# Attention and MoE on one core: all transposes on TensorE as fp32 words of two tokens, streaming key tiles from -60, a new order

## The chip, the cores and the metric

The kernel runs on 1 core of one Trainium2 chip. The metric is the device time of one execution in microseconds (us). Lower is better.

## What is computed

Attention over 4 batches, 8 heads, 768 tokens and 64 columns a head, then a two-layer MLP with a learned negative slope on the 3072 tokens that come out. Heads 0, 2 and 6 are "retrieval" heads: full causal attention. The other five are "streaming" heads: a token sees the first 4 tokens (sinks) and the last 64.

```python
scores = scale * np.matmul(q, k.transpose(0, 1, 3, 2))
causal = rel >= 0                                  # rel = query position - key position
stream_keep = causal & ((pos[None, :] < n_sink) | ((rel >= 0) & (rel < window)))
mask = np.where(retr, causal, stream_keep)         # n_sink 4, window 64
a = softmax(np.where(mask, scores, -1e9))
x = np.matmul(a, v)                                # [B, H, S, D] -> [B*S, H*D] = [3072, 512]
h = x @ w_in                                       # w_in [512, 2048]
out = (np.maximum(h, 0) + alpha * np.minimum(h, 0)) @ w_out    # w_out [2048, 512]
```

## The kernel before, in words

**Segments.** The attention is cut into 16 segments n: batch n // 4 and one of the head pairs `PAIRS = [(2, 6), (1, 5), (0, 4), (3, 7)]`. So n % 4 = 0 has two retrieval heads, n % 4 = 2 one of each kind, the others two streaming heads. The MLP is cut into 8 token tiles t, two for a batch: 512 tokens (t even) and 256 (t odd).

**Items and their order.** All work is cut into named items, and `ORDER` (line 14) is a list of some 1,080 names written out in full. The program is what comes of calling the items in that order. Each engine runs its own instructions in that order, so the list is the order of every queue: TensorE (PE), VectorE (DVE), ScalarE (ACT), GpSimd (POOL) and SyncE (SP), which issues most DMAs. The names are:
- `Lq`, `Lk`, `Lv` n: load q, k, v of a segment (SP; `load_q`, `load_k`, `load_v`). `Cq`, `Ck`, `Cv`: cast to bf16, on the engine that the strings `CQ`, `CK`, `CV` name (V, P, A).
- `Tq`, `Tk` n (`to_array`, line 355): TensorE transposes q and k of a segment into PSUM. `tq`, `tk` (`put_q` line 365, `put_k` line 373): copies from PSUM into `qT` and `kT`, with the tokens put in order.
- `Dq`, `Dk` n (`dma_q` line 321, `dma_k` line 336): the same by DMA transpose, for segments 8 to 15.
- `S` n.hh.m (`S_retr`, `S_stream`): scores of a part of a head. `s`: their exponential on ScalarE. `m`: multiplication by a 0/1 mask on VectorE, for segments 4 to 15; segments 0 to 3 add a mask of -30000 by a matmul with `ident` instead (lines 462 and 501).
- `A` n.hh (`AV`, line 535): the exponentials times v, with a 65th column of ones that gives the row sum. `a` (`AV_out`): division by the sum into `xn`.
- `X` n: `xn` transposed into `xT`, by TensorE for segments 0 to 3 and 15 (`X_pe`, line 574, then `X_out`, the item `x`), by DMA for the others (`X_dma`, line 567).
- `P` t.f (line 588): first MLP layer for a 512-column slice of PSUM; tile 0's first slices are cut by heads (`P0.f.0` to `P0.f.2`). `p` and `g`: the two halves of the slope function, on ScalarE (line 602) and VectorE (line 609).
- `O` t.s.u (line 613): a quarter of the second layer for 128 tokens. `o`: copy on ScalarE and store. `L0` to `L2`: the last 128 tokens, cut by columns (line 636).
- `warm`: matmuls on zeros, which keep TensorE going while it waits.

**Bursts.** For segments 4 to 15 a score matmul isn't issued at once but pooled (`one_score`, line 411), as long as the next names are scores or items that TensorE doesn't run (`beside_burst`). `emit_burst` (line 417) then issues the pool. With at least 576 columns on each head of the pair, the two heads' matmuls use the two row halves of the array at the same time (line 430). Otherwise each runs by itself over all rows (line 423).

**Tiles.** There are three tilings of queries: `FULL` (6 tiles of 128) for pairs of two retrieval heads, `FAR` (7 tiles, starts 0, 128, 252, ... in steps of 124) in batch 0, and `NEAR` (7 tiles, steps of 112) from batch 1 on. A streaming head's key tile holds the 4 sinks and the keys of a query tile. It gets scores for 192 or 176 queries. The transposed output is kept with the tiling's starts. Rows of q and k lie 6 or 2 tokens to a partition in segments 0 to 7 (`row_tokens`), and `put_q` and `put_k` bring them in order with strided copies (`in_order`). In segments 8 to 15 they lie 1 token to a partition. In batch 0 the sinks of v are copied by `sinks` (line 306), later they are loaded by small DMAs.

**PSUM** has 8 banks, which `take` and `give` hand out in the order of their age. In batch 0 the scores go by bank pairs, `SC2 = [(0, 1), (2, 3)]`.

Of the kernel before, what the change touches and what calls it, by code (L numbers as in the profile page):

```python
# [8 lines left out]
AF = mybir.ActivationFunctionType  # L9
# [5 lines left out]
busy zero id warm0 kz3 Lq0.0 sz1 vz2 nms nmr so1 vz0 Lq0.1 Lk1 warm8 warm5 warm3 kz1 qz0 one Lq1 Lk0 La Ck0.0 kz2  # L15
Cq0.0 Tq0.0 tq0.0 Tk0.0 qz warm2 Lk2 kz0 tk0.0 Ck1.0 Ck1.1 Cq0.1 Tk1 S0.0.1 s0.0.1 Tq0.1 S0.0.0 Cq1 warm7 Lv0 tk1.0
sz2 vz1 vz3 Tq1 Lq2 Ck0.1 S0.0.2 s0.0.0 tk1.1 Tk0.1 Ck2.1 tq1 S1.1.0 s0.0.2 Ck2.0 warm4 tq0.1 nz0 s1.1.0 Cq2 tk0.1 Cv0
Lk3 S0.1.0 kfz0 Lv1 vo ro0 Ck3.1 s0.1.0 Lq3 Ck3.0 wi1 wi0 Cq3 sz0 idf S1.0.0 so2 Al s1.0.0 so0 al S0.1.1 s0.1.1 Lv2
Tq2 Tk2 tk2.1 tk2.0 S0.1.2 S1.0.1 A0.0 s0.1.2 a0.0 Cv1 A0.1 a0.1 Cv2 s1.0.1 tq2 S1.1.1 nz1 Tk3 S2.0.1 tk3.0 s1.1.1
S2.0.2 X0 s2.0.1 x0 wi6 s2.0.2 wi7 Lv3 Lq5 Tq3 tk3.1 S2.0.0 wi5 m4.0.2 warm6 S2.1.0 A1.0 a1.0 Lk4 s2.0.0 A2.0 S2.1.1  # L20
A1.1 a2.0 tq3 s2.1.0 a1.1 S3.0.0 s2.1.1 s3.0.0 A2.1 a2.1 S3.1.1 X1 S3.0.1 s3.0.1 Lk5 wi4 kfz2 Cv3.0 Cq5 Lk7 wi2 X2
Ck4.0 s3.1.1 S3.1.0 x1 P0.0.0 x2 P0.0.1 A3.0 P0.1.0 P0.1.1 Lk6 Lq4 Lq6 Ck4.1 kfz3 nr Cv3.1 s3.1.0 A3.1 Lv7 Lv5 Lq7
Ck5.0 wi3 a3.0 P0.2.0 Tq5 tq5 P0.3.0 P0.3.1 a3.1 X3 x3 ns kfz1 P0.2.1 Tk4 near2 P1.2 P0.1.2 P0.2.2 P0.0.2 p1.2 p0.1
g0.1 Ck5.1 P1.0 P0.3.2 g1.2 P0.15 tk4.0 p0.2 g0.2 p0.15 wo0 p1.0 Lk8 near0 g0.15 g1.0 ro1 P1.12 P1.14 m12.1.2 p0.0
g0.0 wo1 tk4.1 p1.12 P0.14 g1.12 p0.14 g0.14 P0.13 p0.13 g0.13 P0.11 p1.14 Tk5 Ck7.1 g1.14 P1.10 tk5.0 p0.11 p1.10
Ck6.0 Ck7.0 g0.11 m8.0.2 tk5.1 wo2 Lv6 Lv4 P0.10 P0.8 p0.8 Tk7 g1.10 wo3 Cq4 Lk9 P0.12 P1.8 p0.10 g0.8 p0.12 g0.10 Tq4
P0.6 P0.9 p0.3 Ck6.1 g0.3 tq4 P0.4.0 P0.5.0 Tk6 P0.4.1 p1.8 g1.8 tk7.0 p0.9 g0.9 Cq6 P0.5.1 P0.5.2 p0.5 g0.12 p0.6
tk6.1 P0.4.2 g0.6 g0.5 tk6.0 S4.0.5 P0.7 p0.7 P1.6 g0.7 P1.4 s4.0.5 p0.4 Tq6 m4.1.2 tk7.1 g0.4 Cv5 p1.6 g1.6 O0.1.0
tq6 S4.0.3 O0.2.0 O0.2.1 S5.1.1 S5.0.0 S4.0.1 S6.1.0 m14.0.2 p1.4 g1.4 s5.0.0 O0.1.1 s4.0.3 s4.0.1 O0.2.2 S5.0.2
S5.1.0 S4.0.2 S5.1.2 s6.1.0 m4.0.1 Cv7 O0.3.0 s5.0.2 s5.1.2 s5.1.1 s4.0.2 O0.1.2 s5.1.0 O0.1.3 o0.1 Cq7 Cv4 O0.3.1  # L30
m5.1.0 m8.1.2 m5.0.2 m4.0.3 m5.1.2 S4.0.0 S4.1.4 S5.0.1 S4.0.4 S4.1.0 s4.0.4 s5.0.1 Lk10 m5.0.1 O0.2.3 O0.3.2 Tq7
m5.0.0 o0.2 s4.1.0 m4.0.4 m5.1.1 A5.1 s4.0.0 m4.0.0 a5.1 O0.3.3 tq7 S7.0.0 S7.0.1 S4.1.3 S7.1.1 S6.0.5 S4.1.1 m4.0.5
s4.1.4 o0.3 Lq9 s4.1.3 Ck8 m4.1.3 A5.0 a5.0 X5 s4.1.1 A4.0 s7.0.0 s7.1.1 Lk11 Lq8 s7.0.1 a4.0 s6.0.5 near1 m7.0.0
m7.1.1 m4.1.0 O1.1.0 S7.1.0 S6.0.4 S7.0.2 S4.1.5 S6.0.1 S7.1.2 S6.1.1 O1.1.1 Cv6 s7.1.0 O1.0.0 s4.1.5 m7.0.1 s6.1.1
m4.1.5 m6.1.1 s7.1.2 m6.1.0 s7.0.2 m7.0.2 S6.0.2 S4.1.2 S6.1.2 S6.0.0 s6.0.4 s4.1.2 s6.0.1 s6.1.2 O1.0.1 m6.0.5 m7.1.0
m4.1.1 m4.1.4 m7.1.2 m6.1.2 S6.0.3 A4.1 s6.0.0 m6.0.0 m6.0.1 A7.1 O1.1.2 A6.1 s6.0.3 m6.0.4 m6.0.3 s6.0.2 a4.1 a6.1
A6.0 A7.0 a6.0 O1.1.3 O0.0.0 O0.0.1 O0.0.2 O1.0.2 m10.0.2 O1.0.3 O0.0.3 o0.0 X4 X6 a7.1 a7.0 X7 P2.9 P2.3 p2.9 P3.4
Ck9 Cq9 g2.9 P2.14 p2.14 g2.14 Cq8 p3.4 Lq10 Lq11 Dk8.0 P2.10 p2.10 Dk9.1 o1.0 p2.3 g2.3 g3.4 Dk8.1 P3.2 P3.14 P3.12
# [24 lines left out]
s15.1.0 m12.1.4 s14.0.2 s15.1.1 m14.1.1 m14.0.5 m14.1.2 m12.1.3 m14.1.0 A12.1 m14.0.3 A14.1 A14.0 a14.0 s15.1.2 a14.1
m15.0.2 s15.0.1 a12.1 O4.1.1 X13 O4.0.0 O4.0.1 O4.0.2 O4.0.3 m15.0.0 m15.1.1 O4.1.2 m15.0.1 m15.1.2 m15.1.0 A15.0 o4.0
A15.1 a15.0 O4.1.3 a15.1 O5.0.2 X15 O5.0.3 X14 x15 o4.1 o5.0 X12 P6.11 p6.11 P6.2 P6.15 P6.10 p6.10 P7.4 P6.0 P6.1
g6.11 g6.10 p6.1 P6.6 P7.8 p6.15 g6.15 g6.1 p6.0 g6.0 P6.5 p7.4 p6.5 p6.6 g7.4 g6.6 g6.5 P6.3 P6.12 P7.2 p6.3 p6.12
g6.12 p6.2 g6.2 P6.4 p7.8 P7.6 P6.14 g6.3 g7.8 p7.6 p6.4 g7.6 g6.4 P7.10 P6.7 P6.8 p6.8 p6.7 P7.0 P6.9 P6.13 g6.7 p7.2
g7.2 g6.8 p7.10 g7.10 p6.9 P7.14 O6.3.0 P7.12 p6.13 g6.13 p7.12 O6.0.0 O6.0.1 O6.1.0 p7.0 g7.0 g6.9 O6.3.1 O7.0.0
O6.3.2 O6.1.1 p7.14 p6.14 g6.14 g7.12 O6.3.3 o6.3 O6.0.2 O6.1.2 O6.1.3 o6.1 O6.0.3 o6.0 O6.2.0 O6.2.1 O6.2.2 O7.0.1
O7.0.2 O6.2.3 o6.2 m12.0.2 g7.14 L2 l2 O7.0.3 o7.0 L0 L1 l1 warm1 l0  # L70
""".split()


@with_exitstack
def kernel(
    ctx: ExitStack,
    tc: tile.TileContext,
    q: bass.AP,
    k: bass.AP,
    v: bass.AP,  # L80
    is_retrieval: bass.AP,
# [14 lines left out]
    bf16 = DT.bfloat16  # L96

    RETR = [1, 0, 1, 0, 0, 0, 1, 0]
    PAIRS = [(2, 6), (1, 5), (0, 4), (3, 7)]
    NSINK = 4  # L100
    NT = 7
    SLOT = 256
    LAY = 4
    CROSS = 8

    class Tiles:

        def __init__(self, starts, masked):
# [13 lines left out]
    def full(n):  # L122
        return all(RETR[h] for h in PAIRS[n % 4])
# [724 lines left out]
```

## Time and profile before

| what | value |
|---|---|
| median of the runs shown (3) | 230.23 us (229.36 to 230.96) |
| profiled execution, its own time | 230.69 us |
| its span, first to last instruction | 229.0 us |
| mean granted TensorE clock | 0.999 |
| DMA, mean | 163 GB/s, 37.39 MB |
| packets under 512 B | 82,440 of 95,417 |
| DMA transposes on SP | 16 of k, 8 of q, 11 of outputs |

The profile shows one execution. PE is TensorE's matmuls, PEld its weight loads, which overlap them. A busy share is the share of the span; matmuls are pipelined, so one that shows 219 ns may be followed by the next after 56 ns. A row of a group gives line, engine, operation, tiles and shape, then busy us and mean ns of one, then the engine's idle time before it and what ended it.

### The profile page before, as it was taken

The numbers are of one execution on the slowest core, as the hardware profiler recorded it, in microseconds if no ns is written. First come the engines' busy times: TensorE is split into PE (matmuls) and PEld (weight loads), VectorE is DVE, ScalarE is ACT, GpSimd is POOL, SyncE is SP. The second block draws the span as 40 slices with busy tenths as digits, with TensorE's granted clock in tenths as the row PEclk, the third lists the DMA queues.
The fourth block names the chain that finished last, engine by engine and source line by source line (L and its number), as shares of the span: only waits on it lengthen the run. The fifth ranks groups of instructions, "written<-read, shape, count | busy, mean of one in ns | idle before, by whom it ended". The sixth has DMA issues, their size and how long they took to land.

```text
span 229.0 us, 5240 instructions
## 1 busy us (share of the span) xinstructions
PE 222.6 (97%) x2005; PEld 136.2 (59%) x2005; DVE 151.3 (66%) x394; ACT 140.9 (62%) x285; POOL 46.0 (20%) x91
## 2 busy tenths in 40 slices
PE   8889999999999999999999999999999999999994
PEld 8779866655465656555556455556556555664454
DVE  6679968976459915899699309986576635966000
ACT  4679629999799127477995127787594236553311
POOL 6589896100040001000300001000110110000000
PEclk9999999999999999999999999999999999999999
DMA  6999999999897698999989799994821420000213
GB/s 192 281 269 215 283 225 271 201 197 238 182 258 183 107 199 216 193 145 191 250 171 219 164 265 146 225 186 95 142 93 38 115 94 0 0 3 1 84 68 124
DMA packets 95417, 37.39 MB, mean 163 GB/s; under 512 B 82440, under 2 KB 93600, under 8 KB 95392
## 3 DMA queue, kind: packets, MB, share of 16 engines
q1 hardware_dynamic: 89136, 27.73, 61.8%
q0 software_dynamic: 5792, 8.93, 17.0%
q10 hardware_dynamic: 464, 0.40, 0.5%
q8 instruction: 15, 0.25, 0.4%
q14 instruction: 10, 0.08, 0.1%
HBM read 27.71 MB, written 6.29 MB: 148 GB/s over the span
## 4 chain that ended last, share of the span: by engine, by line
PE 88%; DVE 4%; ACT 2%; DMA 2%; issue 1%; SPq 1%; POOL 0%; DVEq 0%
PE P L597 35%; PE P L617 34%; PE P L552 7%; PE P L430 4%; DMA kf<-in_k_dram 2%; PE P L363 2%; PE P L413 2%; PE P L636 2%; ACT neg L602 1%; PE P L577 1%; DVE kT L392 1%; DVE vb L306 1%; PE P L501 1%; PE P L423 1%; ACT kT L392 1%
## 5 line engine op out<-in xcount | busy, mean ns | idle before, releaser
L609 DVE SCALAR_TENSOR_TENSOR g<-neg,oma,P 128x256 bf16<-128x256 f32 (+1 forms) x128 | 71.1, 609 | 36.0 <-ACT neg L602 35.5
L597 PE MATMUL P<-xT,w_in_b 128*128 128x512 bf16 (+1 forms) x512 | 86.5, 326 | 0.0
L617 PE MATMUL P<-w_out_b,g 128*128 128x512 bf16 x368 | 85.4, 379 | 0.0
L602 ACT ACTIVATE neg<-P 128x512 f32<-128x512 f32 x96 | 54.1, 599 | 27.1 <-PE P L597 22.6
L597 PEld LDWEIGHTS <-w_in_b 128*128 128x128 bf16 x512 | 49.5, 98 | 31.7 <-DVE g L609 0.2
L617 PEld LDWEIGHTS <-g 128*128 128x128 bf16 x368 | 33.7, 98 | 37.2 <-issue 1.2
L469 ACT ACTIVATE eR<-P 128x448 bf16<-128x448 f32 (+4 forms) x63 | 37.1, 636 | 6.6 <-PE P L462 2.8
L623 ACT COPY ot<-P 128x512 f32<-128x512 f32 x23 | 13.9, 603 | 37.3 <-PE P L617 32.4
L627 POOL DMA_DIRECT2D out_dram<-ot x18 | 10.3, 573 | 115.2 <-ACT ot L623 115.0
L517 ACT ACTIVATE eS<-P 128x352 bf16<-128x352 f32 x45 | 20.9, 494 | 3.7 <-PE P L430 3.7
L563 DVE TENSOR_TENSOR xn<-P,rcp 128x448 bf16<-128x448 f32 (+1 forms) x32 | 19.4, 608 | 1.1
L528 DVE TENSOR_TENSOR eS<-eS,ms_near 128x352 bf16<-128x352 bf16 x45 | 14.3, 335 | 5.0 <-ACT eS L517 4.9
L479 DVE TENSOR_TENSOR eR<-eR,mr_near 128x128 bf16<-128x128 bf16 (+5 forms) x54 | 10.8, 227 | 4.5 <-ACT eR L469 4.5
L430 PE MATMUL P<-qT,kT 64*128 64x176 bf16 (+13 forms) x181 | 11.7, 251 | 0.3 <-DVE g L609 0.3
L430 PEld LDWEIGHTS <-kT 64*128 64x128 bf16 x181 | 7.2, 94 | 7.6 <-issue 6.4
L413 PE MATMUL P<-qT,kT 128*128 128x192 bf16 (+14 forms) x68 | 11.3, 251 | 0.3 <-ACT eS L523 0.3
L552 PE MATMUL P<-vb,eS 128*128 128x65 bf16 x260 | 11.0, 193 | 0.4 <-DVE vb L306 0.4
L552 PEld LDWEIGHTS <-eS 128*128 128x128 bf16 x260 | 9.7, 97 | 2.9 <-issue 1.1
L562 DVE RECIPROCAL rcp<-P 128x7 f32<-128x7 f32 (+1 forms) x32 | 6.3, 197 | 6.2 <-PE P L552 6.0
L552 PE MATMUL P<-vb,eR 128*128 128x65 bf16 x276 | 10.1, 193 | 0.0
L552 PEld LDWEIGHTS <-eR 128*128 128x128 bf16 x276 | 9.4, 97 | 1.2
L645 DVE COPY ot<-P 128x128 f32<-128x128 f32 x1 | 0.3, 292 | 14.3 <-PE P L636 14.3
(96 smaller groups left out, 178.7 us busy)
## 6 DMA issues: line engine op xcount, KB each, us to landing
out_dram<-ot POOLq DMA_DIRECT2D x18, 256.0 KB, 3.4
kf<-in_k_dram SPq DMA_DIRECT2D x21, 192.0 KB
qf<-in_q_dram SPq DMA_DIRECT2D x18, 192.0 KB
vf<-in_v_dram SPq DMA_DIRECT2D x14, 196.0 KB
qf<-in_q_dram SPq DMA_DIRECT2D x7, 384.0 KB
vf<-in_v_dram SPq DMA_DIRECT2D x12, 192.0 KB
w_in_b<-in_moe_w_in_dram POOLq DMA_DIRECT2D x8, 256.0 KB, 8.8
w_out_b<-in_moe_w_out_dram POOLq DMA_DIRECT2D x4, 512.0 KB, 13.7
```

Of the source, the lines that this page charges most:

```text
L413: nc.tensor.matmul(to, keys, queries, start=True, stop=stop)
L430: nc.tensor.matmul(to, keys[own], queries[own], start=True, stop=True)
L469: nc.scalar.activation(ebuf[n, hh][:, lo:hi].rearrange("p (x c) -> p x c", x=len(parts)), P[:, got[0]:got[0] + len(parts), 0:(hi - lo) // ...
L517: nc.scalar.activation(slots, sc[:, 0:352].rearrange("p (s c) -> p s c", c=176), AF.Exp, scale=scale)
L528: nc.vector.tensor_tensor(slots, slots, ms_near[:, 0:2, :] if m == 0 else ms_near[:, 1:3, :], op=ALU.mult)
L552: nc.tensor.matmul(pav[:, i, :], e[:, o:o + 128], vv[:, j, hh, 0:D + 1], start=(m == 0), stop=(m == len(terms) - 1))
L563: nc.vector.tensor_tensor(xn[n][:, 0:nt, D * hh:D * hh + D], pav[:, :, 0:D], rcp.to_broadcast([128, nt, D]), op=ALU.mult)
L597: nc.tensor.matmul(psg[:, w * i:w * (i + 1)], w_in_b[:, c, 128 * fb:128 * (fb + 1)], xT[:, c, o:o + w], start=(x == 0), stop=(x == 3))
L602: nc.scalar.activation(neg[t, f], bank(held["P", t, f][0]), AF.Relu, scale=-1.0)
L609: nc.vector.scalar_tensor_tensor(g_buf[t % 2][:, fb, 0:w], neg[t, f][:, c], oma[:, fb:fb + 1], bank(got[0])[:, c], op0=ALU.mult, op1=ALU.add)
L617: nc.tensor.matmul(bank(held["O", t, s][0]), g_buf[t % 2][:, f, 128 * s:128 * (s + 1)], w_out_b[:, f, :], start=(f == 0), stop=(f == 15))
L623: nc.scalar.copy(ot, bank(got[0]))
```

## The change

- **Words of two tokens.** q, k and the outputs are laid down so that two bf16 tokens of a column lie side by side (`in_pairs`). TensorE transposes them as fp32 words, three transposes a segment where there were six or seven, and their bits come out as two bf16 tokens side by side again. For q and k word i of a partition goes to every third word of PSUM, so that the tokens come out in order and `put_q` and `put_k` are plain copies.
- **No DMA transposes.** `dma_q`, `dma_k` and `X_dma` are gone. Segments 8 to 15 get items `Tq`, `Tk`, `tq`, `tk`, and all segments `X` and `x`. Their casts move from VectorE to POOL; `tq` is on VectorE in batch 0 and on ScalarE after it; `tk` is on VectorE, but on ScalarE in segments 4 to 7.
- **Tiles.** All queries lie in 6 tiles of 128. A streaming key tile j holds the 4 sinks and 124 keys from `KEY0[j]` = -60, 64, 188, ..., and gets scores for up to 188 queries.
- **Loads.** q and k come with 6 tokens to a partition in all segments. The sinks of v are loaded by a small DMA in batch 0 too.
- **Masks and constants** follow the tiles; `ident_f` is now 128x128 and `ident` is made from it.
- **Rows of the outputs** are stored by `out_rows`, 64 rows twice, as the tokens now lie.
- **A new order** of 1,093 names, with 24 matmuls in `warm0` where there were 32.

```diff
-    NEAR = Tiles([112 * i for i in range(NT)], [16 * j + 128 for j in range(6)])
-    FAR = Tiles([0] + [124 * i + 4 for i in range(1, NT)], [128] + [4 * j + 124 for j in range(1, 6)])
-    FULL = Tiles([128 * i for i in range(6)], [128] * 6)
+    KEY0 = [64 - KEYS + KEYS * j for j in range(NT)]
+    QT = [[(j, 128 * i - KEY0[j]) for j in range(NT)
+           if 128 * i - 63 < KEY0[j] + KEYS and KEY0[j] < 128 * (i + 1)] for i in range(6)]
...
-    CQ = "VPPPPPAAVVVVVVVV"
-    CK = "APPPPPVVVVVVVVVV"
+    CQ = "VPPPPPAAPPPPPPPP"
+    CK = "APPPPPVVPPPPPPPP"
...
+    def in_pairs(nat, hh):
+
+        return nat.rearrange("p (i c t) -> p i t c", i=3, t=2)[:, :, :, D * hh:D * (hh + 1)]
...
     def to_array(key, nat, choices, first_half=False):
 
         held[key] = take(*choices)
-        tr = bank_bf(held[key][0])
-        for i in range(6):
-            if first_half:
-                nc.tensor.transpose(tr[0:D, 128 * i:128 * (i + 1)], nat[:, i, 0:D], ident)
-            else:
-                nc.tensor.transpose(tr[:, 128 * i:128 * (i + 1)], nat[:, i, :], ident)
+        words = nat.bitcast(fp32).rearrange("p (i c) -> p i c", i=3)
+        d = D if first_half else 128
+        for i in range(3):
+            nc.tensor.transpose(bank(held[key][0])[0:d, i:i + 382:3], words[:, i, 0:d], ident_f)
 
     def put_q(key, n, rows, copy):
-        tr = bank_bf(held[key][0])
-        T = row_tokens(n)
-        cast_of(copy)(qT[n % NK][rows, 0:S].rearrange("d (p t) -> d p t", t=T), in_order(tr[rows, 0:S], T))
+        cast_of(copy)(qT[n % NK][rows, 0:S], bank_bf(held[key][0])[rows, 0:S])
         give(held.pop(key))
...
-        for i, x in enumerate(tiles(n).QS):
-            nc.tensor.transpose(bank_bf(got[0])[:, x:x + 128], xn[n][:, i, :], ident)
+        words = xn[n].bitcast(fp32).rearrange("p (i c) -> p i c", i=3)
+        for i in range(3):
+            nc.tensor.transpose(bank(got[0])[:, 128 * i:128 * (i + 1)], words[:, i, :], ident_f)
...
-    for i, n in enumerate((32, 3, 14, 4, 4, 4, 4, 4, 4)):
+    for i, n in enumerate((24, 3, 14, 4, 4, 4, 4, 4, 4)):
```

The new order begins and goes on like this on TensorE, up to the first slices of the MLP (other engines' items left out): `warm4 warm5 warm0 warm8 Tk0.0 Tq0.0 Tq0.1 Tk0.1 warm6 S0.0.1 Tk3 S0.1.1 warm2 Tk1 S0.1.2 warm7 Tq1 S0.0.0 S0.1.0 S1.0.0 Tk2 S1.1.0 Tq3 S1.1.1 A0.1 S0.0.2 S1.0.1 Al Tq2 A0.0 S3.0.0 A1.0 S3.0.1 A1.1 S3.1.1 S3.1.0 S2.0.0 X1 S2.0.1 X0 S2.0.2 A3.0 S2.1.0 warm3 A2.0 S2.1.1 A3.1 P0.0.0 A2.1 P0.1.0 X3 P0.3.0 X2 P0.4.0`. On ScalarE the first exponentials come as `s0.1.1 s0.0.1 s0.1.2`, and on SP the loads as `Lq0.0 Lk0 Lq0.1 Lk3 Lk1 Lq1 Lk2 Lq3 Lv0 Lq2`.

## The prediction

> **What bounds the kernel now.** I read the page first, then the chain in order of time, then the groups of TensorE and of its weight loads with the shapes kept apart, then the windows.
>
> ```profile
> PE 222.6 (97%) x2005; PEld 136.2 (59%) x2005; DVE 151.3 (66%) x394; ACT 140.9 (62%) x285; POOL 46.0 (20%) x91
> PE   8889999999999999999999999999999999999994
> PEclk9999999999999999999999999999999999999999
> ```
>
> TensorE works in every slice at the full granted clock, the other engines have a third free or more. So the span is the sum of TensorE's work plus the little that it loses, and a change counts by what it does to that sum. These lines of the chain give the price of one matmul where nothing interrupts:
>
> ```profile
> 15.73 0.67 PE P L363 x12
> 17.30 1.27 PE P L552 x42
> 205.96 15.54 PE P L617 x72
> ```
>
> A 128-column transpose costs 0.67/12 = 56 ns, a 65-column AV matmul 30 ns, a 512-column matmul 216 ns: (columns + 5.5) x 0.417 ns. I summed this over all items of the old order. Two-headed bursts of scores count by their longer half.
>
> In us: P1 83.1, P2 79.4, the last cut tile 3.5, AV 536 x 29.4 ns = 15.7, scores 16.5 (17 bursts 8.7, alone 7.8), added masks 3.5, transposes 142 x 55.6 ns = 7.9; together 209.6, and warm-ups 3.9. TensorE is through near 225.7, so 12.2 us are lost: by differences along the trace about 7.4 before 33 us, 0.24 per burst (17: 4.1), and 0.7 near 50 to 58 us, where ScalarE is late. After it come 3.3 us of copy and store.
>
> The early loss has this look, in the timeline of ScalarE and in the chain:
>
> ```profile
> 9.08 1.75 ACT L469 ACTIVATE eR<-P 128x896 bf16<-128x896 f32 x2 [1.58 <-PE P L462]
> 18.18 0.81 ACT L368 COPY qT<-P 128x768 bf16<-128x768 bf16 x1
> 27.97 0.81 ACT L523 ACTIVATE eS<-P 128x768 bf16<-128x768 f32 x1 [0.53 <-PE P L501]
> ```
> ```profile
> 28.33 1.74 DVE vb L306
> ```
>
> Batch 0's exponentials run from 9.08 to 28.78, 3.6 us of it idle; TensorE gets two score-bank pairs back only as they end. Then a 4-partition sink copy holds VectorE, and A3.1 resumes at 30.11. By then TensorE has done 18.8 us of real work: 11.3 us without.
>
> **TensorE's sum after the change.** P1, P2 and the last tile are the same.
>
> AV: six query tiles in place of seven where a streaming head is in the pair. Streaming heads go from 13 to 12 matmuls (20 heads), retrieval heads of pair (0,4) from 27 to 21 (4 heads): 44 x 29.4 ns = -1.3.
>
> Scores: tiles at -60 give 128 + 5 x 188 + 84 = 1152 columns, as before; retrieval loses 760 columns in all. But the new order pools fewer. Going through it by the rule of emit_burst I find 12 bursts with 26,064 columns (before 17 with 37,768) and 67 matmuls alone for segments 4 to 15 (before 23). Before: 8.67 + 7.83 + 17 x 0.24 = 20.6. After: 6.13 + 12.49 + 12 x 0.24 = 21.5. That is +0.9.
>
> Transposes: 142 bf16 become 150 fp32 (51 q, 51 k, 48 outputs), since a word carries two tokens and a segment needs three where it needed six or seven. The trace has one fp32 transpose, of 16 rows, and one bf16 load without the full 128 columns:
>
> ```profile
> L363 PE MATMUL P<-ident,g 128*128 128x128 bf16 x48 | 3.8, 219 | 0.7 <-DVE kT L394 0.5 <-POOL g L328 0.2
> L651 PE MATMUL P<-ident_f,alpha_r 16*128 16x16 f32 x1 | 0.2, 231 | 0.6 <-DVE eS L288 0.6
> L430 PE MATMUL P<-qT,kT 64*128 64x16 bf16 x3 | 0.5, 180 | 0.0
> ```
> ```profile
> L363 PEld LDWEIGHTS <-g 128*128 128x128 bf16 x48 | 2.9, 97 | 1.1 <-issue 0.6 <-POOL g L328 0.4
> L651 PEld LDWEIGHTS P<-ident_f,alpha_r 16*128 16x128 f32 x1 | 0.1, 134 | 0.9 <-DVE eS L288 0.9
> ```
> ```profile
> L361 PEld LDWEIGHTS <-g x12: 110/140/178, 5.9 to 6.7; 128*64 128x64 bf16 x12
> ```
>
> Loads: 110 ns for 64 slow columns (the fastest of L361), 134 ns for 128 fp32 ones: 0.375 ns a column, so 48 ns for 128, under the 56 ns of the transpose before it that can hide it. The fp32 matmul began with its load, and 231 - 48 = 183 ns is what 16 bf16 columns take (180); four passes would add 20 ns. So I take one pass with the load hidden, 58 ns: 8.7, +0.8 over 7.9. Lower end 55.6 ns (+0.4). Upper ends: load and transpose one after the other, 104 ns (+7.7); four passes, as one 512-column matmul, 216 ns (+24.5).
>
> The Trainium skill speaks against it: TensorE: Matmul & The Clock Gate, section "Weight-path perf modes — Fast Weight Load (FWL) and DoubleRow", says that fast weight load needs an input that isn't FP32. Its section "LDWEIGHTS (loading the stationary operand)" gives columns / 1.2 ns, so 107 ns for 128, and by it the 150 transposes would be an estimated 16.0 us (+8.1). The trace agrees that the load is slower (134 against 97 ns) but not by that much.
>
> Warm-ups: 65 for 73; they run while the first data is on its way, so nothing. TensorE in all: -1.3 + 0.9 + 0.8 = +0.4.
>
> **What the other engines get.** ScalarE copies q for segments 8 to 15 (8 x 0.80, L368) and runs 5 short extra exponentials (0.28 each, L519) in batch 0, but loses three q copies there. VectorE gets 11 output copies (0.55 each, L582) and the keys of segments 8 to 15 (6 x 0.55 and 10 x about 0.76, from L582's 0.7 ns an element), +17.0; it loses their casts (16 x 0.59 = 9.4), +7.6 in all over three batches. 32 casts of 0.51 go to POOL, in whose queue they stand behind output DMAs that wait for ScalarE's copy. If such a cast is late, the transpose behind it stops TensorE, whose queue is in order.
>
> ```profile
> 33.00:83.00 50.00, 49.69 (x449) 28.80 (x447) 35.35 (x102) 39.11 (x88) 9.25 (x18) 1.00 0.99 203
> 83.00:133.00 50.00, 50.00 (x426) 28.39 (x425) 36.73 (x98) 31.41 (x69) 5.36 (x9) 1.00 1.09 199
> ```
>
> The columns from the third on are PE, PEld, DVE, ACT and POOL. VectorE has 13 of 50 us free and would use about 3 of them. Over the new order's stages I compared sums of row durations: from P2.1 to P3.0 TensorE 25.1, VectorE 23.0, ScalarE 18.7; from P4.5 to P5.10 20.6, 18.9, 13.6; so all is covered, and if the cover is gone, each exposed key copy costs 0.76. From P0.0.0 to O1.1.0 the old order gives ScalarE 40.8 us against 38.5 of TensorE, which is the 0.7 loss; the new one reaches O1.1.0 after 22.3 with 17.1. I take 0.4 of the 0.7 as gained.
>
> On SP, 24 DMA transposes of q and k and 11 of outputs go. They waited (L571 on VectorE's xn 14.6 us by the queue's waits) with loads behind them; no TensorE wait names them, so their going is worth nothing by itself. Loads of q and k become rows of 1,536 bytes. Sinks of v come by small DMAs in batch 0 too, which drops the 1.74 us copy.
>
> **The first 30 us.** TensorE has 15.1 us of real work before A2.1, behind the last exponential of batch 0. Those still start near 9.1: S0.1.1, first on ScalarE, waits for segment 3's keys, fourth and fifth on SP (before, the fourth landed at 7.5), two casts of 0.51, three transposes. Busy time then is 16.1 - 3 x 0.7 + 5 x 0.2 = 15.0. With no idle A2.1 comes at 24.4 (9.3 lost, -2.0 against 11.3); with the 3.6 of before at 28.0 (+1.6). VectorE's queue before it is some 4 us shorter (sink copy, interleaved key copies of 0.93 become about 0.7), but v0 lands later (eighth segment load, not sixth), so I take 2.2 idle: 26.6, +0.2.
>
> **Sum.** 0.4 (TensorE) + 0.2 (start) - 0.4 (ScalarE's stage) = +0.2 on a profiled execution of 230.69 (span 229.0, 1.7 around it). The median of the runs shown is 230.23, 0.5 below the profiled one, so 230.4. Within 1% is about what a measurement of this kernel can tell from no change; 227.9 to 232.5 is also this case's own range.
>
> **The rivals.**
> 1. The start runs without idle on ScalarE and its later stage costs nothing: -2.0 - 0.7 + 0.4 = -2.3, with hidden loads at 55.6 ns another -0.4: 227.5. For it: VectorE's queue shrinks and packets grow, where DMA is busiest. Against: one idle time of ScalarE per segment before, each from TensorE.
> 2. Slower: fp32 transposes take 104 ns (load not hidden) or 109 ns (two passes). It decides from 58 + 2300/111 = 79 ns on, where it costs 2.3 us (1%): 111 of the 150 lie behind batch 0. 111 x 46 to 51 ns = +5.1 to 5.7: 235.5 to 236.1. For it: 231 against 180 ns; two passes over 16 columns cost only 7 ns, which one row can't show. Against: the load's 134 ns.
> By columns / 1.2 ns of the Trainium skill's page TensorE: Matmul & The Clock Gate (section "LDWEIGHTS (loading the stationary operand)") it would be an estimated 235.8.
> 3. Hand-offs late: 35 new ones (8 q, 16 k parts, 11 outputs) go through PSUM and a copy before TensorE may go on. If 12 expose half a prelu (0.37) each, +4.4: 234.8, and with four exposed nothing shows. Against it: the stage sums.
> 4. The change doesn't do what it says: a transpose is run as four passes, 111 x 158 ns = +17.5: 248.
>
> **How the numbers follow.** Forecast 0.38, rival 1 0.27, rival 2 0.15, rival 3 0.15, rival 4 0.05. Faster by over 1%: rival 1 and 0.03 of the forecast, 0.30. Slower: rivals 2 to 4, 0.35. Within 1%: 0.35. Range 227.2 (a little below rival 1) to 236.5 (the top of rival 2), which leaves out rival 4 and a better start.
>
> **What would show it.** Transposes of 128x128 f32 starting 56 to 60 ns apart, loads near 134 ns; 492 AV matmuls; A2.1 near 26.8; no slice of TensorE under 9 tenths between 33 us and the last. Wrong if the transposes start over 80 ns apart, if ScalarE's exponentials of batch 0 end by 25 or after 29, or if waits of TensorE on key copies add up to over 2 us.

## The result and the profile after

The changed kernel takes 251.71 us in the median (250.98 to 252.55, 4 runs); the kernel before, run beside it on the same chip, 229.83 (229.36 to 230.96, 4 runs). The ratio is 1.0945, 95% interval 1.089 to 1.1001: 9.4% slower, 15 us above the top of the predicted range. Ratios leave disturbed executions out and medians don't; where the two say different things below, the ratio is used.

From the page of the changed kernel come its engines, TensorE's busy tenths and granted clock in 40 slices of 6.2 us, and the chain by engine (what ended last, followed back from the end):

```profile
PE 234.2 (94%) x1961; PEld 147.0 (59%) x1961; DVE 157.3 (63%) x429; ACT 147.9 (59%) x302; POOL 58.9 (24%) x106
PE   8996259999999999999999999999999999999995
PEclk9999957999999999999999999999999999999999
PE 77%; SPq 10%; DMA 6%; DVE 4%; POOL 1%; issue 1%; ACT 0%; DVEq 0%
```

Two things are new. TensorE has a hole in slices 4 to 6, which none of the lines of before had, and its clock is down just behind it. And SP's queue stands in the chain with 10%, DMA with 6%; before, TensorE had 88% of it and SP 1%.

The groups of TensorE and of its weight loads (count, busy us, mean ns of one) show the new transposes:

```profile
L485 PE MATMUL P<-ident_f,xn 128*128 128x128 f32 x48 | 7.8, 276 | 0.0
L308 PE MATMUL P<-ident_f,natk 128*128 128x128 f32 x36 | 6.0, 275 | 0.0
L467 PE MATMUL P<-vb,eS 128*128 128x65 bf16 x240 | 11.1, 200 | 8.7 <-POOL vb L296 6.5 <-POOL vb L300 2.1
L467 PE MATMUL P<-vb,eR 128*128 128x65 bf16 x252 | 10.1, 197 | 1.1 <-DVE xT L490 1.1
```
```profile
L308 PEld LDWEIGHTS P<-ident_f,natk 128*128 128x128 f32 x36 | 4.4, 141 | 1.5 <-POOL natq L276 0.2
```

One fp32 transpose lasts 275 ns where the bf16 one lasted 219, and from start to start it takes 109 ns (run 1 below), which is what (256 + 5.5) x 0.417 gives for a bf16 matmul of 256 columns. The AV matmuls are 240 + 252 = 492. Their idle time names POOL's casts of v (`vb`), 8.6 us; that is what the hole waits for.

I took the sum over all items again, with 109 ns for a transpose, and set it beside the start times in both traces:

| us | before | after | difference |
|---|---|---|---|
| transposes | 8.0 | 16.5 | +8.5 |
| scores, by columns | 16.5 | 18.6 | +2.1 |
| AV | 15.7 | 14.5 | -1.3 |
| warm-ups | 4.1 | 3.6 | -0.4 |
| all work of TensorE | 213.7 | 222.6 | +8.9 |
| lost, up to the end of batch 0's AV | 7.4 (at 30 us) | 19.3 (at 40 us) | +11.9 |
| lost from there on | 4.8 | 4.1 | -0.7 |
| the end behind TensorE | 3.1 | 3.2 | +0.1 |
| span | 229.0 | 249.2 | +20.2 |

By the ratio the difference is 21.7 us; these two traces are 20.2 apart, as the traced execution of before took 230.69 us, above its median, and that of the changed kernel 250.98, below its own. Two costs stand out: 8.5 us of transposes and 11.9 us at the start. The start is read from the chain in order of time (start, us, what; its sink loads and the load that it ends in):

```profile
10.71 3.96 SPq L209
15.06 2.89 SPq L209
18.91 2.92 SPq L209
22.22 5.69 SPq L209
28.71 6.71 DMA vf<-in_v_dram
```

L209 is the small load of v's sinks, 7 KB, on SP. Each time it holds SP for 2.9 to 5.7 us, right behind the big load of v (124 rows, 217 KB), and everything on SP stands behind it. The waits of TensorE (us in total, times, longest) and the stretches (PE, PEld, DVE, ACT, POOL busy, granted clock, DMA share, GB/s) show what comes of it:

```profile
PE P L467 <- POOL vb L296: 6.5, 1, 6.5
PE P L467 <- POOL vb L300: 2.1, 1, 2.1
```
```profile
26.20:30.00 3.80, 0.25 (x4) 0.13 (x3) 0.00 (x0) 1.21 (x2) 0.00 (x0) 1.00 0.73 120
30.00:40.00 10.00, 5.93 (x68) 5.04 (x67) 3.06 (x8) 1.41 (x3) 3.82 (x6) 0.50 0.72 145
40.00:43.20 3.20, 3.20 (x29) 2.11 (x28) 1.92 (x5) 0.00 (x0) 1.68 (x3) 0.95 1.17 267
```

A3.0 waits for the first head of segment 3 and TensorE stands still for 6.7 us; the second head's v lands at 35.4. Within that gap, near 30 us, the granted clock falls to 0.5, and it stays there for 10.2 us, some 6 of them with work. The extra times between starts are 2.3 us ahead of A1.0, 6.7 ahead of A3.0 and 1.4 ahead of A2.0; of the 4.0 us that are lost between A3.0 and 40.0, 2.6 are left for the lower clock.

### The profile page after: what moved, and what is told of

Read it like the earlier page. It is cut to its first block, busy times and chain, and to the rows that moved or that the text cites. A ratio compares the mean times of both kernels' runs of the same rounds, so it can differ in the third digit from the quotient of the medians.

```text
span 249.2 us, 5160 instructions
## 1 busy us (share of the span) xinstructions
PE 234.2 (94%) x1961; PEld 147.0 (59%) x1961; DVE 157.3 (63%) x429; ACT 147.9 (59%) x302; POOL 58.9 (24%) x106
## 3 DMA queue, kind: packets, MB, share of 16 engines
q0 software_dynamic: 5728, 8.91, 15.5%
## 4 chain that ended last, share of the span: by engine, by line
PE 77%; SPq 10%; DMA 6%; DVE 4%; POOL 1%; issue 1%; ACT 0%; DVEq 0%
PE P L510 32%; PE P L530 29%; SPq L209 6%; PE P L467 5%; DMA vf<-in_v_dram 5%; PE P L308 3%; PE P L369 3%; PE P L362 2%; DMA kf<-in_k_dram 2%; PE P L485 1%; PE P L547 1%; DVE xn L477 1%; SPq L206 1%; DVE eR L415 1%; SPq L201 1%; SPq L189 1%
## 5 line engine op out<-in xcount | busy, mean ns | idle before, releaser
L522 DVE SCALAR_TENSOR_TENSOR g<-neg,oma,P 128x256 bf16<-128x256 f32 (+1 forms) x128 | 71.1, 610 | 39.2 <-ACT neg L515 38.8
L407 ACT ACTIVATE eR<-P 128x448 bf16<-128x448 f32 (+1 forms) x63 | 34.8, 604 | 6.9 <-PE P L400 3.0
L441 ACT ACTIVATE eS<-P 128x376 bf16<-128x376 f32 (+1 forms) x55 | 26.6, 525 | 20.1 <-PE P L430 10.6
L450 DVE TENSOR_TENSOR eS<-eS,ms 128x376 bf16<-128x376 bf16 x45 | 15.8, 368 | 11.5 <-ACT eS L441 11.3
L477 DVE TENSOR_TENSOR xn<-P,rcp 128x384 bf16<-128x384 f32 x32 | 18.9, 591 | 1.1
L276 POOL CAST natk<-kf 128x384 bf16<-128x384 f32 x20 | 12.7, 661 | 9.1 <-DMA kf<-in_k_dram 8.7
L276 POOL CAST natq<-qf 128x384 bf16<-128x384 f32 x20 | 11.5, 623 | 8.8 <-DMA qf<-in_q_dram 5.5
L311 ACT COPY qT<-P 128x768 bf16<-128x768 bf16 (+1 forms) x13 | 10.4, 796 | 4.9 <-PE P L308 4.9
L352 PE MATMUL P<-qT,kT 128*128 128x188 bf16 (+6 forms) x68 | 12.2, 261 | 0.6 <-DVE qT L311 0.5
L415 DVE TENSOR_TENSOR eR<-eR,mr 128x128 bf16<-128x128 bf16 x54 | 10.8, 239 | 0.3 <-ACT eR L407 0.2
L476 DVE RECIPROCAL rcp<-P 128x6 f32<-128x6 f32 x32 | 6.1, 190 | 7.0 <-PE P L467 6.7
## 6 DMA issues: line engine op xcount, KB each, us to landing
w_out_b<-in_moe_w_out_dram POOLq DMA_DIRECT2D x4, 512.0 KB, 11.9
```

The lines of the kernel that those rows point to most:

```text
L276: copy(in_pairs(nat, hh), buf[:, hh].rearrange("p (i t) d -> p i t d", t=2))
L407: nc.scalar.activation(ebuf[n, hh][:, lo:hi].rearrange("p (x c) -> p x c", x=len(parts)), P[:, got[0]:got[0] + len(parts), 0:(hi - lo) // ...
L441: nc.scalar.activation(slots_of(n, hh, m), sc[:, :, 0:2 * WIDE].rearrange("p x (s c) -> p x s c", c=WIDE), AF.Exp, scale=scale)
L450: nc.vector.tensor_tensor(slots, slots, ms[:, 0:2, :] if m == 0 else ms[:, 1:3, :], op=ALU.mult)
L477: nc.vector.tensor_tensor(in_pairs(xn[n], hh), pav[:, :, :, 0:D], rcp.to_broadcast([128, 3, 2, D]), op=ALU.mult)
L522: nc.vector.scalar_tensor_tensor(g_buf[t % 2][:, fb, 0:w], neg[t, f][:, c], oma[:, fb:fb + 1], bank(got[0])[:, c], op0=ALU.mult, op1=ALU.add)
```

## The experiments

**1. The forms by themselves.** A kernel of its own, with groups of 24 transposes of each form (12 in turn with matmuls) and groups of four loads of each form, nothing else running.

```diff
+nc.tensor.transpose(b[:, 0:128], wb, ident)                      # bf16, L51
+nc.tensor.transpose(nxt()[:, 0:128], wf, ident_f)                # fp32, L54
+nc.tensor.transpose(nxt()[0:64, 0:128], wf[:, 0:64], ident_f)    # load of 64 columns, L60
+nc.tensor.transpose(nxt()[:, 0:64], wf[0:64, :], ident_f[0:64, 0:64])   # 64 columns to move, L63
...
+nc.sync.dma_start(buf[i][:, :, 0, :], dram(v, head(h) - 64 * D, [[D, 128], [124 * D, 7], [1, D]]))        # L92
+nc.sync.dma_start(buf[i][4:128, :, 0, :], dram(v, head(h) - 60 * D, [[D, 124], [124 * D, 7], [1, D]]))    # L95
+nc.sync.dma_start(buf[i][4:116, :, 0, :], dram(v, head(h), [[D, 112], [112 * D, 7], [1, D]]))             # L98
+nc.sync.dma_start(buf[i][0:4, :, 1, :], dram(v, head(h), [[D, 4], [0, 7], [1, D]]))                       # L101
```

> A measurement of forms alone; it computes nothing of the reference. TensorE: 24 transposes of each form in a row, banks in turn. Theory 'two passes': an fp32 transpose with 128 moving columns starts 109 ns after the one before it, whatever its load (128 or 64 columns) and whatever step its output has, and with 64 moving columns 56 ns; the plain fp32 matmul of 128 columns about 216 ns (four passes). Theory 'load not hidden' (the other price of rival 2): 104 ns with a load of 128 columns, 80 ns with a load of 64, and 77 ns with 64 moving columns. bf16 transposes 56 ns in both. SP: theory 'the sink DMA is slow by itself': four sink DMAs in a row take about 3 us each on SP; theory 'the 124-row load is slow to be described and the next DMA bears it': four of these take 3 us or more each from the second on, four sink DMAs in a row 0.4 us each, and a sink DMA after loads of q's form 0.4 us.

TensorE's groups:

```profile
L54 PE MATMUL P<-ident_f,wf 128*128 128x128 f32 x24 | 2.8, 272 | 0.0
L60 PE MATMUL P<-ident_f,wf 128*64 128x128 f32 x24 | 2.8, 273 | 0.0
L63 PE MATMUL P<-ident_f,wf 64*128 64x64 f32 x24 | 1.7, 225 | 0.0
L51 PE MATMUL P<-ident,wb 128*128 128x128 bf16 x24 | 1.5, 219 | 0.0
```

24 fp32 transposes take 2.8 us, 24 bf16 ones 1.5: with the last one's length taken off, (2.8 - 0.27)/23 = 109 ns against 56. With half the columns to load (L60) nothing changes, and in turn with 512-column matmuls, under which a load has 216 ns to hide, a pair takes 109 + 216. So the load is hidden, and the transpose itself takes as long as two passes of bf16. A plain fp32 matmul of the same size takes 224 ns in two records, as long as four. With 64 columns to move (L63) it is 63 ns, where two passes would take 56. What adds 7 wasn't tried; loads of 128 and of 64 columns last 140 and 111 ns, so one of 128 is an estimated 58 ns by its columns and may show there.

SP's issues of the four forms over the whole kernel (ns shortest, median, longest), and the stretches in which the groups of four are on the way (us, PE, PEld, DVE, POOL busy, granted clock, DMA share, GB/s):

```profile
L92 SPq DMA_DIRECT2D b<-in_v_dram x6: 367/368/379, 52.5 to 100.0; - x6
L95 SPq DMA_DIRECT2D b<-in_v_dram x6: 252/1149/3082, 60.1 to 90.8; - x6
L98 SPq DMA_DIRECT2D b<-in_v_dram x4: 313/316/318, 75.4 to 78.2; - x4
L101 SPq DMA_DIRECT2D b<-in_v_dram x10: 249/275/2670, 82.2 to 111.2; - x10
```
```profile
55.50:59.00 3.50, 0.00 (x0) 0.00 (x0) 0.40 (x3) 0.00 (x0) 0.50 0.80 178
62.00:74.00 12.00, 0.00 (x0) 0.00 (x0) 1.27 (x4) 0.00 (x0) 0.50 0.31 70
78.30:81.00 2.70, 0.00 (x0) 0.00 (x0) 0.31 (x2) 0.00 (x0) 0.50 0.70 160
```

Four loads of 124 rows in a row take SP 0.33, 1.97, 2.92 and 3.08 us; each of 128 or 112 rows takes 0.31 to 0.38. The loads of 124 rows land 3.07 us apart, at 70 GB/s, and at most 7 packets are on the way at a time. Those of 128 rows land 1.0 apart, at 178 GB/s, with up to 25 packets; they were issued 0.94 apart, as VectorE cleared their buffers, so they may go faster than that. The sink load costs SP 0.25 us behind others of its kind, but 1.96 and 2.67 behind a load of 124 rows, and 0.28 behind one of 128: the DMA that comes next on SP bears the slow one. This form was the unnoticed part of the change.

The Trainium skill's page DMA: Bandwidth & Descriptors, section "Why a DMA increments its semaphore by 16 and not by 1", says that a copy is spread over the largest number of engines, up to 16, that divides the slowest dimension of source and destination; for 124 rows that is 4, for 112 and 128 rows 16. The semaphore events of the trace agree: as a load of 124 rows lands, its semaphore gets 4 updates, at one of 128 or 112 rows 16, and at one of 12 rows 12 (run 5). The rate falls by less than from 16 to 4: from 178 to 70 GB/s. By that rule the form could have been told from the others ahead of any run, though not its price. Which four engines carried the packets isn't in the trace.

**2. The sinks on another queue.** In batch 0 the sink loads are issued by POOL, not SP.

```diff
-nc.sync.dma_start(dst[0:NSINK, :, hh, :], ...)
+(nc.gpsimd if n < 4 else nc.sync).dma_start(dst[0:NSINK, :, hh, :], ...)
```

> The changed kernel with the sink DMAs of batch 0 issued from POOL's queue instead of SP's. Theory 'the sink DMA holds SP': SP is free of some 20 us of issue in batch 0, A3.0 no longer waits, the loss before A2.1 falls from about 20 us to 9 to 11, and the time from 251.7 to 240 to 243. Theory 'the 124-row load is what is slow': the next DMA on SP bears the same time, and it stays at 249 to 252. Theory 'the DMA engines are the limit': also 249 to 252.

251.7 us (251.06 to 253.06), ratio 1.0963 (1.0909 to 1.1017): nothing gained. Its chain has the next DMAs of SP where the sinks were:

```profile
10.84 4.01 SPq L206
14.90 3.07 SPq L201
18.71 3.38 SPq L206
```

L206 is the next head's 124-row load, L201 a 128-row one. The line that the chain names for the delay isn't the line that makes it.

**3. 128 rows in batch 0, the sinks aside.** The v loads of batch 0 bring 128 rows from token -64; the sinks go to an unused tile, so their values are missing in that batch.

```diff
+if n < 4:
+    nc.sync.dma_start(dst[:, :, hh, :], dram(v, o + (KEY0[0] - NSINK) * D, [[D, 128], [KEYS * D, NT], [1, D]]))
+    nc.sync.dma_start(aside[hh], dram(v, o, [[D, NSINK], [0, NT], [1, D]]))
+    continue
```

> The changed kernel with v of batch 0's streaming heads loaded in one DMA of 128 rows, the sink DMAs still on SP but into a tile that nothing reads: the sinks' values are left out of batch 0. Theory 'the sink DMA holds SP': about 249 to 252, as the changed kernel. Theory 'the 124-row load is what is slow': 240 to 243, and the sink DMAs take under 1 us each on SP.

242.98 us (one run), span 241.3, TensorE's clock at full speed up to the last matmuls. The lost time at 30 us is 10.4, and no wait of TensorE is longer than 3.0 us.

**4. 128 rows in batch 0, the sinks copied by POOL.** As 3, with the right values by a copy.

```diff
+vh = vb[n % NV][:, :, hh, 0:D].bitcast(fp32)
+nc.gpsimd.tensor_copy(vh[0:NSINK, 1:7, :], vh[64:64 + NSINK, 0:1, :].to_broadcast([NSINK, 6, D // 2]))
```

> The changed kernel with v of batch 0's streaming heads loaded in one DMA of 128 rows and the sinks copied by POOL, as the kernel before does. Both theories on SP: 239 to 242, that is the kernel before plus 8.5 (150 transposes at 109 ns against 142 at 56), with the start about as before. If the time stays over 247, the lateness of v isn't SP's issue but DMA bandwidth.

245.37 us (244.33 to 246.29), ratio 1.0679 (1.0617 to 1.0741). 3 us more than both theories gave, and 2.4 more than run 3. TensorE's longest waits:

```profile
PE P L521 <- DMA w_in_b<-in_moe_w_in_dram: 3.7, 2, 2.3
PE P L478 <- POOL vb L310: 1.7, 1, 1.7
```

The copies stand in POOL's queue, and with them its casts of v and the loads of `w_in` that it issues; that these waits come of the copies is argued, not tried.

**5. 112 + 12 rows.** The smallest edit that touches nothing but the form, in all batches.

```diff
-nc.sync.dma_start(dst[NSINK:128, 0:nt, hh, :], dram(v, o + KEY0[0] * D, [[D, KEYS], [KEYS * D, nt], [1, D]]))
+for a, z in ((16, 128), (NSINK, 16)):
+    nc.sync.dma_start(dst[a:z, 0:nt, hh, :], dram(v, o + (KEY0[0] + a - NSINK) * D, [[D, z - a], [KEYS * D, nt], [1, D]]))
```

> Each load of 124 rows of v (partitions 4 to 127) is issued as two: 112 rows (16 to 127) and 12 rows (4 to 15). Same data, same tiles, same order, nothing copied by an engine, in all batches. Theory A (a DMA of 124 rows is slow by its row count, and the next DMA on SP bears it): the loads of v land about 1 us apart, A2.1 comes before 31 us instead of 40, and the time is 242 to 245 us. Theory B (the loads of v are late for their place in the queue or their 256-byte rows): the number of packets and the order are the same, so the time stays at 250 to 253. If A holds, what is left over the kernel before (12 to 15 us) is 8.9 us of TensorE work and up to 6 us of other waits.

241.79 us, ratio 1.0524 (1.0504 to 1.0544). That is 1.0945 x 229.83 - 1.0524 x 229.49 = 10.0 us less than the changed kernel, just below theory A's 242 to 245. Of its page, and of SP's loads of v (count: ns shortest, median, longest):

```profile
PE   7899799999999999999999999999999999999994
PEclk9999999999999999999999999999999999999999
```
```profile
L207 SPq DMA_DIRECT2D vf<-in_v_dram x40: 317/500/5622, 9.7 to 130.7; - x40
L210 SPq DMA_DIRECT2D vf<-in_v_dram x20: 253/303/1079, 11.9 to 131.3; - x20
```

The sink loads (L210) last 0.30 us in the median; in the changed kernel they lasted 2.90, and 13.8 at the longest. The time lost by 35 us is 9.0, all through 13.9 against 12.2 before. What is left, 240.0 - 229.0 = 11.0 us of span, is 8.9 of work, 1.7 lost and 0.4 at the end. (By the ratio it is 12.0 us.)

**6. The slow form put into the kernel before.** The five loads of 128 rows of its batch 0 are issued as 124 + 4 rows.

```diff
-nc.sync.dma_start(dst[:, 0:nt, hh, :], dram(src, o, [[D, 128], [step * D, nt], [1, D]]))
+for a, z in ((NSINK, 128), (0, NSINK)) if nt == 7 else ((0, 128),):
+    nc.sync.dma_start(dst[a:z, 0:nt, hh, :], dram(src, o + a * D, [[D, z - a], [step * D, nt], [1, D]]))
```

> The other part alone, made to the kernel before: the five v loads of batch 0 that bring 128 rows x 7 tiles for a streaming head are issued as two, 124 rows (partitions 4 to 127) and 4 rows; same data, same place in the order. Theory A (the form of 124 rows is slow in any kernel): each takes 3 us or more instead of 1, v lands late, the idle time before A3.1 grows, and the time is 4 to 12 us longer, 234 to 242. Theory B (the start of the changed kernel was late because of its order, and the split only helped it): within 1 us.

244.65 us, ratio 1.0686 (1.0628 to 1.0744): some 16 us, more than either theory gave, from the form of five loads. Here the queue holds up casts of q and k too; TensorE's waits and the page:

```profile
PE P L364 <- POOL g L316: 8.3, 1, 8.3
PE P L364 <- POOL natq L316: 2.4, 1, 2.4
```
```profile
PE   8991496699999999999999999999999999999995
PEclk9999579589999999999999999999999999999999
```

The same picture as in the changed kernel: a hole of 8 us with a lower clock behind it, and here the clock stands at 0.5 twice, for 10.2 us from 23.4 on and for 6.8 us from 43.9 on. So part of the 16 us is the lower clock.

**7. A third of the output transposes.** From here on the base is the kernel with 112 + 12 rows. Two of three transposes of each segment's outputs are left out.

```diff
-for i in range(3):
+for i in range(1):
     nc.tensor.transpose(bank(got[0])[:, 128 * i:128 * (i + 1)], words[:, i, :], ident_f)
```

> The kernel with 112 + 12 rows, and of the three transposes of each segment's outputs only the first is done; the copy after it writes its result three times (so 2 of 3 output blocks of each segment are left out of the result; VectorE's copy stays as long). 32 of 150 transposes go. Theory A (109 ns each, and all on the path): 3.5 us faster than the kernel with 112 + 12 rows, 2.6 if those of batch 0 lie in idle time. Theory B (the prediction's 58 ns each): 1.4 to 1.9 us faster. Theory C (the time is set elsewhere, by the hand-offs): under 1 us.

Ratio 1.0442 (1.042 to 1.0464) against 1.0524: 1.9 us. That would fit the price of 58 ns, but the trace doesn't: work falls by 32 x 109 = 3.5, and the lost time grows from 13.9 to 15.5, by 1.0 in batch 0 and by 0.6 behind it. The outputs' transposes lie at the ends of the score stages; that something else is nearly as late there is likely, but wasn't tried.

**8. The transposes of q and k twice.** In segments 4 to 15, into the same place.

```diff
-for i in range(3):
+for i in list(range(3)) * (2 if key[0] in ("q", "k") and key[1] >= 4 else 1):
     nc.tensor.transpose(bank(held[key][0])[0:d, i:i + 382:3], words[:, i, 0:d], ident_f)
```

> The kernel with 112 + 12 rows, and every transpose of q and k in segments 4 to 15 is done twice into the same place: 72 fp32 transposes more, same result. Theory A (109 ns each, all on the path, also in the stages between the expert matmuls): 72 x 109 ns = 7.8 us slower than the kernel with 112 + 12 rows, 249 to 250. Theory B (58 ns each, as predicted): 4.2 us slower, about 246. Theory C (part of it lies in waits that are there anyway, as the gain from leaving out output transposes did): 4 to 6.5 us slower.

Ratio 1.0974 (1.0906 to 1.1043): 10.3 us over the base's 1.0524, and at least 8.3 from the upper end of the base's interval, 1.0544. The spans of the profiled executions are 247.2 and 240.0, 7.2 apart. The two don't agree closely, but both are nearer to 72 x 109 ns = 7.8 than to 4.2. These transposes lie among the MLP's matmuls, and their full length counts.

**9. The outputs as bf16.** Six bf16 blocks for three of fp32 words, segments 4 to 15; token order and stores follow.

```diff
+for i in range(6):
+    nc.tensor.transpose(bank_bf(got[0])[:, 128 * i:128 * (i + 1)], xn[n][:, 128 * i:128 * (i + 1)], ident)
```

> The kernel with 112 + 12 rows, and the outputs of segments 4 to 15 are transposed as bf16, six blocks of 128 columns for three of fp32 words. Theory A (an fp32 transpose is two passes): 72 x 55.6 ns = 4.0 us for 36 x 109 ns = 3.9 us, so the time is the same within 0.5 us. Theory B (one fp32 transpose costs 58 ns, as predicted, and its time comes from elsewhere): 36 x 53 ns = 1.9 us slower.

241.7 us, ratio 1.0511 (1.0473 to 1.055): the same as 1.0524. Two tokens to a word save instructions, not time.

**10. The outputs by DMA again, in the new order.** Segments 4 to 14; segment 15 by six bf16 transposes, and token order and stores as in 9.

```diff
+nc.sync.dma_start(xT[:, heads(n)[0], o:o + S].rearrange("p (i r) -> p i r", r=128), xn[n], transpose=True)
```

> The kernel with 112 + 12 rows, and the outputs of segments 4 to 14 go to xT by a DMA transpose on SP, as in the kernel before (segment 15 by six bf16 transposes on TensorE); their 33 fp32 transposes and 11 copies on VectorE go. Theory A (what the change gave up is TensorE time, which DMA transposes did not take): 33 x 109 ns = 3.6 us faster than the kernel with 112 + 12 rows, so 238.5 to 241. Theory B (the DMA transposes' own waits on SP hold the loads behind them, which is why they were worth removing): less than 1.5 us faster, or slower.

246.55 us, ratio 1.078 (1.0705 to 1.0854): 5.9 us slower than the base, though TensorE has 3.6 us less to do. The waits:

```profile
PE P L525 <- DMA xT<-xn: 5.8, 3, 3.1
```

The new order puts the last outputs of a batch right ahead of the MLP that reads them; by DMA they come up to 3.1 us late, and behind that wait the clock stands at 0.5 for 3.4 us. So the DMA transposes can't be had back without an order that gives them time.

**11. The outputs on TensorE, in the old order.** One part of the change, made to the kernel before.

```diff
-item(f"X{n}", X_dma, n)
+item(f"X{n}", lambda n=n: (X_pe(n), X_out(n)))
```

> One part of the change alone, made to the kernel before: the outputs of segments 4 to 14 are transposed on TensorE (bf16, six or seven blocks of 128 columns, 74 in all) and copied by VectorE, and their 11 DMA transposes go; loads and order are as before. Theory A (a DMA transpose costs TensorE nothing where the order gives it time, so moving it to TensorE costs its full length): 74 x 55.6 ns = 4.1 us slower than the kernel before, 233 to 234. Theory B (TensorE waits on the DMA transposes about as long as it would need to do them): within 1 us.

241.91 us, ratio 1.054 (1.051 to 1.057): 12.3 us by the medians, three times the work moved. Of 10.4 us between the profiled spans 74 x 55.6 ns = 4.1 are work; TensorE's waits and its clock are the rest:

```profile
PE P L577 <- DVE xn L563: 4.2, 3, 2.3
PE P L597 <- DVE xT L582: 1.2, 1, 1.2
```

In the old order an output transpose stands right behind the division that makes its input. In the kernel before, SP's queue waits there for `xn` (14.6 us) and no wait of TensorE names it; here TensorE itself waits, with everything that stands behind in its queue. Right behind the wait of 2.3 us the granted clock stands at 0.5 for 3.4 us, all of them with work, which is another 1.7. Neither theory had this.

**12. The new tiles alone.** The old order with keys from -60 and six query tiles, DMA transposes where they were, loads as 112 + 12 rows. The heart of it, shortened:

```diff
-to_array(("k", n), natk[n], two)                       # the changed kernel, segments 8 to 15
+nc.sync.dma_start(kTs[n % NK][hh][:, 0:128 * nt].rearrange("p (i r) -> p i r", r=128),
+                  natk[n][:, 896 * hh:896 * hh + 128 * nt], transpose=True)   # q and the outputs likewise
```

> What the runs leave of the change as worth having: the old order with the new tiles (keys of 124 from -60, six query tiles of 128), fp32-word transposes only where the kernel before transposed on TensorE (segments 0 to 7, outputs of batch 0), DMA transposes for the rest as before, and every load of 124 rows issued as 112 + 12. By the sum over all items TensorE has 211.4 us of work against 213.7 before (AV -1.3, scores -0.2, transposes -0.3, warm-ups -0.4 that count for nothing). Theory A (the span follows that sum, since the start is as before): 1 to 2.3 us faster than the kernel before, 227.2 to 228.7. Theory B (the start of the new tiles, with their three v loads per head and the masks added on POOL, costs what the sum gains): 229 to 232.

231.86 us, ratio 1.0098 (1.0068 to 1.0129): 1% slower, although TensorE has 211.4 us of work for 213.7. It loses 15.5 us in all, 3.3 more than before: half of that by 35 us, where A2.0 waits for v,

```profile
PE P L496 <- POOL vb L329: 1.8, 1, 1.8
```

and the rest behind it, the most of it in the stages of scores and AV. Those get shorter by their AV and are then held elsewhere; by what wasn't tried. No version here beats the kernel before.

## Why the prediction was wrong, point by point

**The transposes, +0.8: wrong, +8.5.** The failed step is "I take one pass with the load hidden, 58 ns". The load was hidden as said (141 ns a load, and half a load changes nothing, run 1), though its 48 ns by columns came from rows of two types; run 1's rows give the estimated 58; what was missed is the second pass. The only fp32 row of the trace had 16 columns, where a second pass is 7 ns, and I let that row decide what it couldn't. Rival 2 had the right price of 109 ns, but counted 111 of 150 transposes, and its argument against, "the load's 134 ns", says nothing of passes. By its price and 150 transposes the term would have read +8.5, as measured, and the time 238.1. The rule of the Trainium skill's page TensorE: Matmul & The Clock Gate, section "LDWEIGHTS (loading the stationary operand)", gave an estimated 16.0 us for all, near the 16.5 measured, but for a cause that run 1 excludes: a load of half the columns leaves the 109 ns as they are.

**The start, +0.2: wrong, +11.9.** A2.1 came at 39.9, not 26.8. The failed step is "Sinks of v come by small DMAs in batch 0 too, which drops the 1.74 us copy": the step moved to loads of 124 rows beside the sinks, and I costed only what it removed. No row of before has a load of 124 rows; its 128-row and 112-row loads were the nearest, and I took theirs without saying so. A form without a row needed a lower and an upper end, and I gave it neither. Runs 5 and 6 show it from both sides: -10.0 us with the form taken out of the changed kernel, some +16 with it put into the kernel before. Run 2 excludes the sink load itself. "v0 lands later (eighth segment load, not sixth)" looked at v for the wrong reason: v0 has 128 rows, landed by 13.8 and no wait of TensorE names it; the late loads were those of segments 1 and 3. Of the start's loss 1.6 us are left in run 5 (9.0 for 7.4), and their cause stays open.

**The clock: not foreseen.** 2.6 of the 11.9 us are TensorE at a lower clock behind its own hole, so a wait of 6.7 us cost 9.3. Run 6 has the same pair, a hole and a lower clock; runs 3 and 5, whose waits are 3.0 us at most, keep the clock in batch 0.

**AV, -1.3: right.** 492 matmuls, 14.5 us. But run 12 shows that a gain in these stages needn't reach the end.

**Scores, +0.9, and ScalarE's stage, -0.4: about right.** By the sum over the new trace's columns the scores got 2.1 longer. The time lost behind batch 0 falls by 0.7, where five fewer bursts (1.2) and ScalarE's stage were to bring 1.6. From 45 to 65 us, where ScalarE's stage lies, nothing is lost any more; the missing 0.9 lies in the score stages behind it, in which no single wait is over 0.5 us.

**The other engines at nothing: right.** VectorE's and POOL's added copies and casts cost nothing that shows: 8.6 us of the waits named POOL, but only because it waited for v. Rival 3, late hand-offs, didn't happen in the new order, which leaves room between a division and its transpose; in the old one it would have (run 11).

**The DMA transposes: half right.** "Their going is worth nothing by itself" holds as far as SP goes: no run shows a gain from it. Of their return in the new order the price is 5.9 us (run 10), of their going in the old one 12.3 (run 11): each order is built for the engine that does them.

**The range.** Its top was rival 2 alone. Two independent costs came together, one priced on too few instructions and one not priced, and no rival joined two. "No slice of TensorE under 9 tenths between 33 us and the last" and "wrong if the transposes start over 80 ns apart" both caught it: 109 ns, and a slice of 5 tenths from 31.1 to 37.4 us. So did the end of ScalarE's exponentials of batch 0, at 39.2 and not by 29.

## What to carry to other kernels

Cost a DMA by its form, not its bytes: a row count that the trace doesn't show is an unknown with two ends, even when it is only four rows off a known one, and a DMA that lasts long on SP may be bearing the one ahead of it. Before packing two bf16 values into an fp32 word to halve TensorE's instructions, time one full-width fp32 transpose: here it took as long as the two it replaced. And work that moves from a queue which may wait to an engine which may not needs the order rebuilt around it, in both directions (runs 10 and 11).

## What was not expected of the hardware

- A load of 124 rows x 7 x 256 bytes runs at 70 GB/s; of 128 rows, issued 0.94 us apart, at 178 or more, of 112 rows at 160 or more (run 1); issued as 112 + 12 rows, the same bytes cost SP a median of 0.5 us a piece (run 5).
- A full fp32 transpose takes 109 ns, bf16 56, a plain fp32 matmul of that size 224; 64 columns of fp32 take 63 (run 1).
- Some 4 us into a gap of 6.7 us TensorE's granted clock fell to 0.5 and stayed there for 10.2 us; the work in them took 2.6 us longer. The length of the gap alone doesn't tell: waits of 2.3 us (run 11) and 3.1 us (run 10) brought 3.4 us at 0.5, one of 2.3 us in run 4 and one of 3.0 us in run 3 none.
